# Attention in steps of a head pair: half-height score tiles, odd value windows copied on the chip, all local evacuations on ScalarE

## The chip, the cores and the metric

The kernel runs on one core of one Trainium2 chip. The metric is the device time of one execution in microseconds, as the median of several runs; the profile is one further execution, recorded by the hardware profiler. A core has TensorE (PE in the profile, with its weight loads as PEld), VectorE (DVE), ScalarE (ACT), GpSimd (POOL) and SyncE (SP), which issues the DMAs here. Matrix products go into PSUM, which has eight banks of 512 fp32 numbers per partition; PE writes them, and VectorE and ScalarE read them out ("evacuate" them) into SBUF.

## The reference

Eight batches of eight heads; 512 local and 32 global tokens; head dimension 64. Global queries attend to everything, local queries to the 32 global keys and to local keys at most 32 positions away. The result is reordered to 4352 rows of 512 and goes through a mixture of eight experts with a greedy assignment.

```python
s_g = scale * np.matmul(q_g, k_all.transpose(0, 1, 3, 2))
out_g = np.matmul(sm(s_g), v_all)
s_ll = scale * np.matmul(q_l, k_l.transpose(0, 1, 3, 2))
mask = np.abs(pos[:, None] - pos[None, :]) <= window      # window = 32
s_ll = np.where(mask, s_ll, -1000000000.0)
s_lg = scale * np.matmul(q_l, k_g.transpose(0, 1, 3, 2))
out_l = np.matmul(sm(np.concatenate([s_lg, s_ll], axis=-1)), np.concatenate([v_g, v_l], axis=2))
...
for e in range(E):                                        # after the greedy assignment
    h = np.maximum(x[mask] @ w1[e], 0.0)
    out[mask] = h @ w2[e]
```

`sm` is a softmax with the row's maximum subtracted.

## The kernel before

The program has two stages: `attention` (lines 64 to 376), which writes its result x to the DRAM tensor `xd` and the gate's logits to `L`, and then routing and `experts` (from line 687). Only the first stage and the host's layout of its inputs (`_layout`, line 961) are touched by the change.

The 512 local queries of a head are cut into 16 blocks (windows) of 32. With the global keys woven in between the local ones (`_blocks`), the keys that a block may see are 128 neighbouring columns, starting at 32 * ((3j + 1) // 2) for block j. So the scores of a block are a 32x128 tile. The host ships for each of the 32 (batch, head pair)s a tensor `qk` with the transposed queries (544 columns) and keys (864 columns) of two heads, one head on partitions 0 to 63 and one on 64 to 127, and a tensor `vw` with the values of all 16 windows of both heads, 128 keys on the partitions, 65 columns each (the 65th is ones and yields the softmax's sum). Neighbouring windows overlap, so most values are shipped more than once.

`load_qk` (line 75) loads q and k in two DMAs; `spread` (line 83) copies q into `qz`, in which the two heads' queries stand on the diagonal of zeros, so that one product over all 128 partitions gives the scores of one block of both heads (64 rows). GpSimd makes these copies, VectorE at the very start. `load_v` (line 89) loads the values in four DMAs.

The work is done in units. A `Local` unit is half of a head pair: eight blocks of both heads. A `Glob` unit is the 32 global queries of four heads. A unit has these parts:

- `a`: the scores. Local: eight products on 128x64 tiles of the array (two column halves, L136). Global: L197, of 512 and of 32 columns.
- `e`: the mask is added and the row maximum taken (VectorE, L143), the maximum is scaled by a small operation (L145), then the exponential (ScalarE, L147). Global: maxima L203 to L205, exponentials L212 to L218.
- `c`: the probabilities are transposed on PE (L152, global L226) into a bank called T, and `evac` copies them to SBUF; of each five copies (`nev`) three go to ScalarE (L253) and two to VectorE (L255).
- `d`: the outputs on 128x32 tiles (L164, global L236) into a bank called O, then VectorE divides by the sum (L167, L168, L172; global L239 to L243). After the last unit of a batch SP writes the batch to `xd` (L175); global rows go by L245.

PSUM is dealt out by names: S for scores with three banks, T with three, O with two. A tile of a name waits until the tile that had its bank three (or two) before was read.

The order is written out by hand. Line 340 runs over the units with a look-ahead of three: `a` and `e` of unit i + 3, `c` of unit i, `d` of unit i - 2; in even steps scores stand first and outputs last on PE, in odd steps the other way round, so that two units' scores and two units' outputs stand side by side. A batch has ten units: eight local and two global. Between them stand the gate's parts (`extra`): `gate_x` transposes x (L261), `gate_m` multiplies with the gate's weights (L267), `gate_l` transposes back and sums into `L` (L276, L277). Loads are issued up to four head pairs ahead; each engine's queue, SP's too, runs strictly in the order of the program, and a load waits on SP until its buffer is free. `rt.prepare` (line 432) makes tables for the routing on VectorE, once, early in attention.

Of the kernel before, what the change touches and what calls it, by code (L numbers as in the profile page):

```python
# [8 lines left out]
F32 = mybir.dt.float32  # L9
# [18 lines left out]
NZ = 6  # L28
# [36 lines left out]
def attention(ctx, tc, A, consts, xd, ident, L, nbatch, rt=None):  # L65
# [6 lines left out]
    G = [(b, g) for b in range(nbatch) for g in range(2)]  # L72
    qk, vw, xs = {}, {}, {}

    def load_qk(b, p):
        t = ld.tile([128, KW], F32, name="qk", bufs=5)
        q = ld.tile([128, QW], F32, name="q", bufs=3)
        z = qz[(b * NP + p) % NZ]
        nc.sync.dma_start(q, A["qk"][b, p, :, :QW])
        nc.sync.dma_start(t, A["qk"][b, p, :, QW:])  # L80
        qk[b, p] = t

        def spread(eng):
            for h in range(2):
                r = slice(64 * h, 64 * h + 64)
                eng.tensor_copy(z[r, :, h, :], q[r].rearrange("p (j i) -> p j i", i=32))  # L86
        return spread

    def load_v(b, p):
        t = ld.tile([128, 2, NW, D + 1], F32, name="vw", bufs=7)  # L90
        f, n = t.rearrange("p h w d -> p (h w d)"), NW * (D + 1) // 2
        for k in range(4):
            nc.sync.dma_start(f[:, k * n:k * n + n], A["vw"][b, p, :, k * n:k * n + n])
        vw[b, p] = t

    qz = [ac.tile([128, QW // 32, 2, 32], F32, name=f"qz{i}") for i in range(NZ)]
    pg = [ac.tile([128, 6, 128], F32, name=f"pg{i}") for i in range(3)]
    mask = ac.tile([128, 2 * NB, 128], F32, name="mask")
    wg = ac.tile([128, 4, 32], F32, name="wg")
    P = [(b, p) for b in range(nbatch) for p in range(NP)]  # L100

    warm = ac.tile([128, 128], F32, name="warm")
# [4 lines left out]
    for i in range(NZ):  # L107
        nc.gpsimd.memset(qz[i][64:128, :, 0, :], 0.0)
        nc.gpsimd.memset(qz[i][0:64, :, 1, :], 0.0)
    for i in range(3):  # L110
        nc.gpsimd.memset(pg[i], 0.0)
    load_qk(0, 0)(nc.vector)
    nc.sync.dma_start(mask.rearrange("p a b -> p (a b)"), A["mask"])
    nc.sync.dma_start(ident, A["ident"])
    spread1 = load_qk(0, 1)
    load_v(0, 0)
    nc.sync.dma_start(wg.rearrange("p a b -> p (a b)"), A["wg"])
    load_qk(0, 2)(nc.gpsimd)
    load_v(0, 1)

    class Local:
        def __init__(s, b, u):
            s.b, s.q, s.u = b, u // 2, u % 2

        def a(s):
            b, q = s.b, s.q
            z = qz[(b * NP + q) % NZ]
            kw = qk[b, q]
            st = ps.tile([128, NB, 128], F32, name="S", bufs=3)
            s.p = wk.tile([128, NB, 128], F32, name="p", bufs=5)  # L130
            s.nm = wk.tile([128, NB], F32, name="nm", bufs=6)
            for c in range(NB):
                for r in range(2):
                    j = 8 * s.u + 2 * c + r
                    k0 = 32 * ((3 * j + 1) // 2)
                    nc.tensor.matmul(st[64 * r:64 * r + 64, c, :], z[:, j].rearrange("p h i -> p (h i)"),  # L136
                                     kw[:, k0:k0 + 128], start=True, stop=True)
            s.st = st

        def e(s):  # L140
            st, nm = s.st, s.nm
            for c in range(NB):
                nc.vector.tensor_tensor_reduce(s.p[:, c, :], st[:, c, :], mask[:, 4 * s.u + c, :], 1.0, -BIG,  # L143
                                               ALU.add, ALU.max, nm[:, c:c + 1])
            nc.vector.tensor_scalar(nm, nm, -SCALE, None, op0=ALU.mult)  # L145
            for c in range(NB):
                nc.scalar.activation(s.p[:, c, :], s.p[:, c, :], AF.Exp, bias=nm[:, c:c + 1], scale=SCALE)  # L147
# [29 lines left out]
    class Glob:  # L177
        def __init__(s, b, g):
            s.b, s.g = b, g
# [845 lines left out]
```

## Time and profile before

| What | Value |
|---|---|
| median of 3 runs | 738.86 us (738.28 to 739.7) |
| the profiled execution's own time | 739.46 us |
| its span, first to last instruction | 737.7 us |
| mean granted TensorE clock | 0.972 |
| PE busy | 686.9 us (93%) |
| VectorE busy | 504.9 us (68%) |
| ScalarE busy | 313.6 us (43%) |
| GpSimd busy | 162.5 us (22%) |
| DMA moved | 120.53 MB, mean 163 GB/s |

A row of a timeline gives start and duration in microseconds, engine, line, operation, output<-inputs, shapes and how many instructions were merged; for a matrix product the shape is rows*columns of the array's tile and then partitions x columns of the moving operand. Durations of matrix products are modelled and overlap; from one run's start to the next one's is what a run costs PE. A fp32 product is two instructions on PE, a transpose is one. A row of a group of instructions gives busy microseconds and the mean nanoseconds of one, then the idle time of its engine before them and what ended it.

### The profile page before, as it was taken

The numbers are of one execution on the slowest core, as the hardware profiler recorded it, in microseconds if no ns is written. First come the engines' busy times: TensorE is split into PE (matmuls) and PEld (weight loads), VectorE is DVE, ScalarE is ACT, GpSimd is POOL, SyncE is SP. The second block draws the span as 40 slices with busy tenths as digits, with TensorE's granted clock in tenths as the row PEclk, the third lists the DMA queues.
The fourth block names the chain that finished last, engine by engine and source line by source line (L and its number), as shares of the span: only waits on it lengthen the run. The fifth ranks groups of instructions, "written<-read, shape, count | busy, mean of one in ns | idle before, by whom it ended". The sixth has DMA issues, their size and how long they took to land.

```text
span 737.7 us, 21308 instructions
## 1 busy us (share of the span) xinstructions
PE 686.9 (93%) x8672; PEld 564.7 (77%) x8672; DVE 504.9 (68%) x1848; ACT 313.6 (43%) x849; POOL 162.5 (22%) x191
## 2 busy tenths in 40 slices
PE   8889999999996279999999999999999999999997
PEld 7677777877773169768878978977977877987985
DVE  5887877977887788866777777776786865550410
ACT  4656756666662034234334333343332433541520
POOL 5222212212100040141042043034024025312002
PEclk9989999999998579999999999999999999999999
DMA  9988998999921061171081072054045055522001
GB/s 324 387 310 296 361 305 300 328 323 306 334 80 60 1 236 55 45 263 45 1 289 62 1 263 89 1 202 148 3 135 200 16 171 192 163 73 89 16 16 46
DMA packets 46242, 120.53 MB, mean 163 GB/s; under 512 B 8256, under 2 KB 8512, under 8 KB 42048
## 3 DMA queue, kind: packets, MB, share of 16 engines
q1 hardware_dynamic: 35904, 67.78, 26.5%
q0 software_dynamic: 10240, 51.39, 19.8%
q8 instruction: 68, 1.11, 0.6%
q14 instruction: 30, 0.25, 0.1%
HBM read 101.32 MB, written 17.83 MB: 162 GB/s over the span
## 4 chain that ended last, share of the span: by engine, by line
PE 45%; DVE 5%; DMA 2%; issue 2%; ACT 1%; POOL 0%; POOLq 0%; DVEq 0%; ACTq 0%
PE Y L903 21%; PE H L875 17%; PE R L485 3%; PE H L747 2%; DVE w2l L417 2%; PE Y L893 2%; DMA w1r<-in_w_dram,widx 1%; DVE r_G L417 1%; ACT w2h L724 1%; DMA xg<-xd,idx 1%; DVE hl L417 0%; DVE r_pm L417 0%; POOL xg L708 0%; PE Y L909 0%; DMA out_dram<-y,idx 0%
## 5 line engine op out<-in xcount | busy, mean ns | idle before, releaser
L875 PE MATMUL H<-xh,w1h 128*128 128x272 f32 x512 | 151.5, 296 | 1.8 <-DVE hl L417 1.4
L875 PE MATMUL H<-xh,w1l 128*128 128x272 f32 x512 | 150.0, 293 | 0.0
L875 PE MATMUL H<-xl,w1h 128*128 128x272 f32 x512 | 149.9, 293 | 0.0
L147 ACT ACTIVATE p<-p,nm 128x128 f32<-128x128 f32 x256 | 81.7, 390 | 65.9 <-DVE nm L145 54.1
L877 ACT ACTIVATE hh<-H 128x272 fp32r<-128x272 f32 x128 | 50.9, 398 | 130.2 <-PE H L875 125.8
L903 PE MATMUL Y<-w2h,hh 128*128 128x512 f32 x256 | 103.9, 406 | 0.0
L903 PE MATMUL Y<-w2l,hh 128*128 128x512 f32 x256 | 102.7, 401 | 0.0
L903 PE MATMUL Y<-w2h,hl 128*128 128x512 f32 x256 | 102.4, 400 | 0.0
L875 PEld LDWEIGHTS H<-xh,w1h 128*128 128x128 f32 x512 | 96.4, 188 | 5.2 <-DVE hl L417 2.4
L875 PEld LDWEIGHTS H<-xl,w1h 128*128 128x128 f32 x512 | 96.5, 188 | 0.6
L875 PEld LDWEIGHTS H<-xh,w1l 128*128 128x128 f32 x512 | 96.4, 188 | 0.3
L86 POOL COPY qz<-q 64x544 f32<-64x544 f32 x60 | 39.2, 654 | 150.3 <-DMA q<-in_qk_dram 108.1
L136 PE MATMUL S<-qk,qz 128*64 128x128 f32 x1024 | 68.5, 284 | 3.1 <-DVE qz L86 2.4
L754 POOL DMA_INDIRECT out_dram<-y,idx x40 | 41.1, 1027 | 136.4 <-ACT y L845 79.3
L417 DVE SCALAR_TENSOR_TENSOR hl<-H,hh 128x272 fp32r<-128x272 f32 x128 | 54.4, 433 | 23.6 <-ACT h L879 12.7
L143 DVE CUSTOM_DVE_ANT_0 p<-S,mask 128x128 f32<-128x128 f32 x256 | 58.8, 285 | 14.9 <-PE S L136 10.5
L417 DVE TENSOR_TENSOR w2l<-w2r,w2h 128x512 fp32r<-128x512 f32 x64 | 43.1, 686 | 37.3 <-ACT w2h L724 37.0
L136 PEld LDWEIGHTS S<-qk,qz 128*64 128x64 f32 x1024 | 58.5, 142 | 10.1 <-issue 6.6
L708 POOL DMA_INDIRECT w1r<-in_w_dram,widx x16 | 15.6, 977 | 221.1 <-DVE r_a L417 124.5
L845 ACT ACTIVATE y<-Y 128x512 f32<-128x512 f32 (+1 forms) x40 | 23.2, 594 | 91.9 <-PE Y L903 70.1
L903 PEld LDWEIGHTS Y<-w2h,hh 128*128 128x128 f32 x256 | 48.2, 188 | 15.7 <-issue 5.9
L724 ACT ACTIVATE w1h<-w1r 128x512 fp32r<-128x512 f32 x64 | 36.4, 622 | 50.4 <-DVE L L417 29.9
(168 smaller groups left out, 1205.9 us busy)
## 6 DMA issues: line engine op xcount, KB each, us to landing
vw<-in_vw_dram SPq DMA_DIRECT2D x128, 260.0 KB, 5.8
qk<-in_qk_dram SPq DMA_DIRECT2D x32, 432.0 KB, 5.8
q<-in_qk_dram SPq DMA_DIRECT2D x32, 272.0 KB, 5.2
xd<-xs SPq DMA_DIRECT2D x8, 1024.0 KB, 7.8
xd<-xg SPq DMA_DIRECT2D x64, 8.0 KB, 4.8
xg<-xd,idx POOLq DMA_INDIRECT x40, 3.6
out_dram<-y,idx POOLq DMA_INDIRECT x40, 2.8
mask<-in_mask_dram SPq DMA_DIRECT2D x1, 512.0 KB, 6.3
```

Of the source, the lines that this page charges most:

```text
L86: eng.tensor_copy(z[r, :, h, :], q[r].rearrange("p (j i) -> p j i", i=32))
L136: nc.tensor.matmul(st[64 * r:64 * r + 64, c, :], z[:, j].rearrange("p h i -> p (h i)"), kw[:, k0:k0 + 128], start=True, stop=True)
L143: nc.vector.tensor_tensor_reduce(s.p[:, c, :], st[:, c, :], mask[:, 4 * s.u + c, :], 1.0, -BIG, ALU.add, ALU.max, nm[:, c:c + 1])
L147: nc.scalar.activation(s.p[:, c, :], s.p[:, c, :], AF.Exp, bias=nm[:, c:c + 1], scale=SCALE)
L417: return op(*args, **kw)
L485: s.nc.tensor.matmul(out, *args, **kw)
L724: nc.scalar.activation(hi, raw, AF.Copy)
L754: nc.gpsimd.indirect_dma_start(out=out, out_offset=bass.IndirectOffsetOnAxis(ap=rt.idx[ph][:n, t:t + 1], axis=0), in_=y[:n], in_offset=None)
L845: nc.scalar.activation(y[:n], p[:n], AF.Copy)
L875: nc.tensor.matmul(p, w[d][:, fs], x[:, d, q], start=(d + k == 0), stop=(d + k == 5))
L877: nc.scalar.activation(hh[:, f, q], p, AF.Relu)
L903: nc.tensor.matmul(p, h[:, f, q], w[f], start=(f + k == 0), stop=(f + k == 9))
```

## The change

A unit becomes a whole head; the work goes in steps of a head pair (five steps to a batch: four local pairs and one of the two global units), with a look-ahead of two steps.

- Scores: `qz` and its copies go. Each head is multiplied for itself on tiles of 64 rows and 32 columns, the two heads alternating, each head into its own S bank: 32 products a pair in place of 16. The global scores are made the same way by `glob_scores`, 512 columns into two S banks, 32 columns into an S bank for the first head and a T bank for the second.
- Maxima: scores are scaled by -SCALE as the mask is taken and the minimum is kept, so that it is the bias of the exponential as it stands (which has scale -1); the small scaling operation goes. The mask is half as large, as a bank now holds one head.
- Values: the host ships the even windows alone, in two DMAs; the odd ones are put together by four GpSimd copies from the even ones, moved by 32 or 64 partitions.
- Evacuations: local and global transposes and the gate's product go to ScalarE, the gate's transposed x to VectorE.
- Buffers: seven for qk (queries and keys in one tile), seven for the values, seven for p, five for pt, and more for small tiles.
- Order within a step: loads; scores of step i + 2; transposes and evacuations of step i, head by head; masks and exponentials of step i + 2; outputs and normalisation of step i - 1; a gate part.

```diff
     def load_v(b, p):
-        t = ld.tile([128, 2, NW, D + 1], F32, name="vw", bufs=7)
-        f, n = t.rearrange("p h w d -> p (h w d)"), NW * (D + 1) // 2
-        for k in range(4):
-            nc.sync.dma_start(f[:, k * n:k * n + n], A["vw"][b, p, :, k * n:k * n + n])
+        t = ld.tile([128, 2, 2, NW // 2, D + 1], F32, name="vw", bufs=7)
+        ev, od = t[:, 0], t[:, 1]
+        n = NW // 2
+        for h in range(2):
+            nc.sync.dma_start(ev[:, h].rearrange("p w d -> p (w d)"), A["vw"][b, p, :, h * n * (D + 1):(h + 1) * n * (D + 1)])
+        nc.gpsimd.tensor_copy(od[0:64], ev[64:128])
+        nc.gpsimd.tensor_copy(od[64:96], ev[32:64])
+        nc.gpsimd.tensor_copy(od[96:128, :, :n - 1], ev[64:96, :, 1:])
+        nc.gpsimd.tensor_copy(od[96:128, :, n - 1:], ev[64:96, :, n - 1:])
         vw[b, p] = t
...
+        def mask(s):
+            s.p = wk.tile([128, NB, 128], F32, name="p", bufs=7)
+            s.nm = wk.tile([128, NB], F32, name="nm", bufs=8)
             for c in range(NB):
-                nc.vector.tensor_tensor_reduce(s.p[:, c, :], st[:, c, :], mask[:, 4 * s.u + c, :], 1.0, -BIG,
-                                               ALU.add, ALU.max, nm[:, c:c + 1])
-            nc.vector.tensor_scalar(nm, nm, -SCALE, None, op0=ALU.mult)
+                nc.vector.tensor_tensor_reduce(s.p[:, c, :], s.st[:, c, :], mask[:, c, :], -SCALE, BIG,
+                                               ALU.add, ALU.min, s.nm[:, c:c + 1])
+        def exp(s):
             for c in range(NB):
-                nc.scalar.activation(s.p[:, c, :], s.p[:, c, :], AF.Exp, bias=nm[:, c:c + 1], scale=SCALE)
+                nc.scalar.activation(s.p[:, c, :], s.p[:, c, :], AF.Exp, bias=s.nm[:, c:c + 1], scale=-1.0)
...
+    def local_scores(u):
+        t = qk[u[0].b, u[0].q]
+        for x in u:
+            x.st = ps.tile([128, NB, 128], F32, name="S", bufs=3)
+        for c in range(NB):
+            for r in range(4):
+                j = 4 * c + r
+                k0 = QW + 32 * ((3 * j + 1) // 2)
+                for h in range(2):
+                    e = slice(64 * h, 64 * h + 64)
+                    nc.tensor.matmul(u[h].st[32 * r:32 * r + 32, c, :], t[e, 32 * j:32 * j + 32], t[e, k0:k0 + 128],
+                                     start=True, stop=True)
...
+    def glob_scores(u):
+        b = u[0].b
+        for x in u:
+            x.sa = ps.tile([128, 512], F32, name="S", bufs=3)
+        for x, n, k in zip(u, "ST", (3, 3)):
+            x.sb = ps.tile([128, 32], F32, name=n, bufs=k)
...
+    nev = dict(p=0, g=0, x=0, l=0)
+    who = dict(p="A", g="A", x="D", l="A")
...
+    LA = 2
+    for i in range(-LA, ns + 1):
...
+        if nx:
+            (local_scores if isinstance(nx[0], Local) else glob_scores)(nx)
+        if cur:
+            cur[0].turn()
+        if cur:
+            cur[0].take()
+        if cur:
+            cur[1].turn()
+        if cur:
+            cur[1].take()
+        if nx:
+            nx[0].mask()
+        if nx:
+            nx[1].mask()
+        if nx:
+            nx[0].exp()
+        if nx:
+            nx[1].exp()
+        if old:
+            old[0].out()
+        if old:
+            old[0].norm()
+        if old:
+            old[1].out()
+        if old:
+            old[1].norm()
+        for f in extra.get((i, 0), []):
             f()
```

Here `nx`, `cur` and `old` are steps i + 2, i and i - 1.

## What was predicted before the run

> **What bounds the kernel now.** The page comes first: how long, which engine is busy, and where.
>
> ```profile
> span 737.7 us, 21308 instructions
> PE   8889999999996279999999999999999999999997
> DMA  9988998999921061171081072054045055522001
> ```
>
> A slice is 18.4 us. In the first twelve (0 to about 221 us) PE and the DMA engines are both at nine tenths; then follow the routing (a hole of PE) and the experts. The diff touches attention alone, so the rest is taken as unchanged. For attention's rhythm I read the timeline of SP's queue: one write of a finished batch to xd each time round.
>
> ```profile
> 75.53 0.38 SPq L175 DMA_DIRECT2D xd<-xs  x1
> ...
> 182.64 0.38 SPq L175 DMA_DIRECT2D xd<-xs  x1
> ```
>
> These are the second and the sixth of eight, so four batches took 107.1 us: **26.8 us a batch**. Whether PE or the loads set that is read from PE's own timeline inside one batch (start, duration, shape, count).
>
> ```profile
> 102.20 0.66 PE L152 MATMUL T<-ident,p 128*128 128x128 f32 x4
> 102.69 0.60 PE L261 MATMUL T<-ident,xs 128*128 128x128 f32 x4
> 103.22 1.97 PE L136 MATMUL S<-qk,qz 128*64 128x128 f32 x32
> 105.12 0.88 PE L226 MATMUL T<-ident,pg 128*128 128x128 f32 x6
> 105.92 1.11 PE L164 MATMUL O<-vw,pt 128*32 128x65 f32 x64
> 106.97 0.66 PE L152 MATMUL T<-ident,p 128*128 128x128 f32 x4
> ...
> 108.91 1.12 PE L197 MATMUL S<-qk,qz 128*64 128x512 f32 x8
> 109.96 0.66 PE L152 MATMUL T<-ident,p 128*128 128x128 f32 x4
> 110.55 0.88 PE L236 MATMUL O<-vw,pgt 128*32 128x64 f32 x48
> 111.25 0.64 PE L164 MATMUL O<-vw,pt 128*32 128x65 f32 x32
> ...
> 123.19 1.07 PE L267 MATMUL O<-xt,wg 128*32 128x512 f32 x8 [0.80 <-DVE gm L239]
> 124.19 1.17 PE L197 MATMUL S<-qk,qz 128*64 128x512 f32 x8
> ```
>
> Each run starts as the one before ends: PE is one dense chain, and the only long pause here is the 0.80 us that the row at 123.19 names. From start to start: scores of a pair (32 instructions) 1.90 us; eight transposes (102.20 to 103.22) 1.02; outputs of a pair (64) 1.05; a gate's four transposes 0.53; scores of one global unit 1.05; its transposes 0.80; its outputs 0.70; the gate's product 1.00. So **PE sets the batch**, and time taken out of PE's chain shortens it until the next engine is reached. The loads are close behind:
>
> ```profile
> DMA packets 23458, 44.52 MB, mean 318 GB/s; under 512 B 4293, under 2 KB 4293, under 8 KB 23425
> ...
> vw<-in_vw_dram SPq DMA_DIRECT2D x88, 260.0 KB, 5.6
> qk<-in_qk_dram SPq DMA_DIRECT2D x22, 432.0 KB, 5.2
> q<-in_qk_dram SPq DMA_DIRECT2D x22, 272.0 KB, 5.0
> ```
>
> That is the DMA view of 55 to 195 us. A pair loads 4 x 260 + 432 + 272 = 1744 KB.
>
> **The change part by part.** *Scores.* Before, a pair has 16 products on 128x64 tiles, two side by side, 32 instructions in 1.90 us. After, it has 32 products on 64x32 tiles: 64 instructions of the same 128 columns, over eight tiles. If all eight run side by side, 64 x (1.90/32) x 2/8 = 0.95 us. No row of this trace has a tile of fewer than 128 rows, so this is bounded: 0.95 from below (nothing makes one instruction shorter), 1.90 from above if only the four column tiles overlap and the row halves take turns. I take 1.05, the row of outputs: the same 64 instructions with 32-column weights. Global scores: two units at 1.05 become one run of half as many streamed columns per tile and twice the tiles, a quarter of 2.1, so 0.53, plus a start; I take 0.75 (bound 1.2).
>
> *The rest of PE's chain* is regrouped but not shortened: per pair 1.02 for transposes and 1.05 for outputs. Per batch PE then has four pairs at 1.05 + 1.02 + 1.05 = 3.12, so 12.5; the global step 0.75 + 2 x 0.75 (transposes) + 2 x 0.75 (outputs) = 3.75; the gate 4 x 0.6 (0.53 and a start, as each stands alone now) + 1.0 + 0.5 (four transposes back) = 3.9. Together **20.1 us**, against 26.8.
>
> *A new wait.* The small global scores of the second head now sit in a T bank, and T has three. That step also takes two T banks for its own transposes, and in it stands a gate unit's transposes, which need the fourth and so wait for ScalarE's last exponential of the second global head. ScalarE's rows give the price.
>
> ```profile
> 102.79 1.28 ACT L147 ACTIVATE p<-p,nm 128x128 f32<-128x128 f32 x4 [1.55 <-DVE ls L167]
> 103.97 0.57 ACT L253 ACTIVATE pt<-T 128x512 f32<-128x512 f32 x1
> 104.45 0.58 ACT L253 ACTIVATE xt<-T 128x512 f32<-128x512 f32 x1
> ...
> 112.37 0.56 ACT L212 ACTIVATE pg<-S,gm 128x384 f32<-128x384 f32 x1
> ...
> 113.53 0.60 ACT L253 ACTIVATE pt<-T 128x512 f32<-128x512 f32 x1
> ```
>
> An evacuation takes 0.48, a global unit's exponentials 1.16, four local ones 1.18. In that step PE has scores until 0.75, transposes until 1.8, outputs until 2.8, and then the gate. ScalarE evacuates until about 2.6 and exponentiates until 2.6 + 2 x 1.16 = 4.9; with the hops, the gate starts at 5.1 rather than 2.8. Behind it on PE stand the next pair's scores, so the chain waits **2.3 us** a batch (bounds 0 and 2.3; I take 2.3, since PE is in order). Then the batch is 20.1 + 2.3, and with 0.3 for pauses like today's **22.7**.
>
> *The engines that could take over.* ScalarE now evacuates all local and global transposes: per pair 2 x 1.18 + 2 x 0.48 = 3.3, four pairs 13.3, a global step 2 x 1.16 + 4 x 0.48 = 4.2, the gate 0.6: 18.1 a batch. For VectorE and GpSimd:
>
> ```profile
> L143 DVE CUSTOM_DVE_ANT_0 p<-S,mask 128x128 f32<-128x128 f32 x164 | 37.7, 286 | 6.6 <-PE S L136 5.4 <-ACT xt L253 1.2
> L86 POOL COPY qz<-q 64x544 f32<-64x544 f32 x40 | 25.5, 637 | 104.0 <-DMA q<-in_qk_dram 74.5 <-PE O L164 10.0 <-PE S L197 6.5
> L255 DVE COPY pt<-T 128x512 f32<-128x512 f32 x16 | 11.0, 686 | 3.3 <-PE T L152 2.9 <-PE T L261 0.4
> L203 DVE TENSOR_REDUCE gm<-S 128x1 f32<-128x512 f32 x10 | 6.9, 686 | 3.9 <-PE S L197 3.9
> ```
>
> ```profile
> 133.51 0.15 DVE L167 TENSOR_SCALAR ls<-O 128x4 f32<-128x4 f32 x1
> ...
> 134.25 0.15 DVE L167 TENSOR_SCALAR ls<-O 128x4 f32<-128x4 f32 x1
> ```
>
> VectorE: eight masks at 0.286 and two normalisations at 0.74 are 3.8 a pair, 15.1 for four; four gate copies 2.7; the global step 2 x (0.69 + 0.4 + 0.75), 3.7: 21.5 at most, since neighbours overlap. Its evacuations and the scaling of the maxima go; they were off PE's chain, so that gives room and no time. GpSimd: 544 elements took 0.637, 1.17 ns each; the four copies of a pair have 1040 + 1040 + 910 + 130 = 3120 elements a partition, 3.7 us, 14.6 a batch, beside PE and four pairs ahead of use. Were it later, outputs would wait. Bounds: 3.7, and twice that, since no copy here moves partitions. I take 3.7. The loads: 4 x 1224 KB, and 1088 KB for xd, are 6.1 MB, at 318 GB/s 19.3 us. SP also holds a value load until the global outputs free four tiles at once, some two steps; the next batch's need is three steps off. All stay under 22.7.
>
> *GpSimd against VectorE.* One VectorE operation shows what a GpSimd copy can do to it:
>
> ```profile
> L145 DVE TENSOR_SCALAR nm<-nm x64: 169/170/706, 9.1 to 219.4; 128x4 f32<-128x4 f32 x64
> ```
>
> Median 170 ns, worst 706, near the 637 of the qz copy that then runs. The change removes this operation, but `prepare` has over a dozen VectorE instructions inside SBUF, which now meet copies of 1.2 us. Bounds 0 and about 12 x 0.6 = 7 us, once; I take 2. The Trainium skill, "SBUF — State Buffer", section "Who interferes with whom", says that a VectorE copy or scalar operation in a two-port mode and a GpSimd instruction exclude each other for a whole instruction. By that rule the price is real and grows with copy length, near the upper bound; on the row above the trace agrees, though the median says that most are not hit.
>
> *Start.* Ahead of the third pair's qk go 256 KB less of mask and 520 KB less of values: 0.78 MB at 318 GB/s, 2.4 us earlier. The spreads and memsets of qz go too, hidden behind that. The tail's gate copies all go to VectorE: +0.5.
>
> **Sum.** Eight batches at 22.7 - 26.8 = -4.1: -32.8; start -2.4; prepare +2; tail +0.5: -32.7. On the profiled execution's own 739.46 us that gives 706.8; it stands 0.6 over the median of 738.86, so about 706.5. I say **707**.
>
> **The rivals.** *PE alone.* The T bank comes free in time or its wait is made up: the batch is 20.1, 2.3 x 8 = 18 us less plus pauses, **686**. For it: bounds as above; against: ScalarE's sum leaves little to make up with.
>
> *Row halves take turns.* The scores stay at 1.90 a pair and 1.2 for the global: +0.85 x 4 + 0.45 = +3.9, the batch is 26.6, **737**. Here the change does not do what it says. For it: no row shows two row tiles; against: column tiles do overlap, two in L136 and four in L164.
>
> *Evacuation binds.* If neighbours on ScalarE stop overlapping (0.39 for an exponential, 0.58 for a copy), its batch is 4 x (3.1 + 1.2) + 4.6 + 0.6 = 22.3, VectorE's 21.5, and engines that wait on one another in order lose some 10%: 24.5, **721**. The Trainium skill, "TensorEngine Tiling (Array Packing)", section "PSUM Bottleneck", says that tiling speeds up TensorE but not the copies out of PSUM, and advises both engines for them; the change goes to one. Today's trace can't show it, as PE is the bound.
>
> *GpSimd binds, slower than before.* If copies to other partitions take 2.2 times the qz rate, a pair needs 8.0 us, a batch 32, and outputs wait for odd tiles: +5.2 x 8, **780**. It decides from 26.8/4 = 6.7 us a pair, 1.8 times. Against it: the qz copies hardly vary, and start and end on quarters of the partitions as these do.
>
> **How the numbers follow.** A measurement can tell about 0.2%, 1.5 us. Chances: forecast 0.50 (696 to 718), PE alone 0.14, evacuation 0.14, row halves 0.12 (a third of it within 0.2%), GpSimd 0.07, some other slower wait 0.03. Faster 0.86, same 0.04, slower 0.10. The range reaches from PE alone, 684, to row halves, 737: about 0.17 stay outside.
>
> **What would show it.** Right: in PE's timeline a pair's 64 score instructions take about 1.05 us start to start; xd writes come 22.7 us apart; once a batch PE pauses some 2 us before the gate's transposes, with ScalarE's exponentials as the releaser; GpSimd copies of about 1.2 us. Wrong: score runs of 1.9; PE pausing at outputs for GpSimd; ScalarE without gaps; SP holding loads so long that scores wait for qk.

## The result, and the profile after

The changed kernel takes 743.84 us (median of 20 runs, 740.12 to 748.0), the kernel before 738.96 us on the same chip (20 runs, 736.99 to 742.07): a ratio of 1.0071, 95% interval 1.0055 to 1.0086. It is **slower by 0.7%**, where 707 us were forecast. Below, the top of its page, with PE's and the DMA engines' slices.

```profile
span 742.2 us, 23504 instructions
PE 667.9 (90%) x9824; PEld 543.8 (73%) x9824; DVE 480.3 (65%) x1762; ACT 320.1 (43%) x867; POOL 220.2 (30%) x247
PE   7788889888697259999999999999999999999997
DMA  9665864876622052081072063044035044522001
```

Attention still fills the first twelve slices. But PE, mostly at nine tenths there before, is now mostly at eight, and the DMA engines fell from nine tenths, after the first slice, to between two and eight. No engine is full, and the stage is no shorter. SP's timeline gives the second and the sixth write of a batch:

```profile
73.66 1.35 SPq L157 DMA_DIRECT2D xd<-xs  x1
...
182.49 0.56 SPq L157 DMA_DIRECT2D xd<-xs  x1
```

(182.49 - 73.66) / 4 is 27.2 us a batch, against 26.8 before and 22.7 forecast. So the expected gain is not given back later; it does not show in these four batches. The first batch is written sooner than before (46.06 us for 50.53), and from the first write to the last it takes 186.7 us (to 232.80) for 179.9 (to 230.43). PE's timeline of one stretch says where it goes:

```profile
98.55 0.87 PE L169 MATMUL S<-qk 64*32 64x128 f32 x40
99.99 0.64 PE L169 MATMUL S<-qk 64*32 64x128 f32 x24 [0.56 <-issue]
100.56 1.09 PE L132 MATMUL T<-ident,p 128*128 128x128 f32 x8
101.58 1.12 PE L143 MATMUL O<-vw,pt 128*32 128x65 f32 x64
102.63 0.66 PE L274 MATMUL T<-ident,xs 128*128 128x128 f32 x4
...
104.13 0.22 PE L248 MATMUL T<-qk 64*32 64x32 f32 x3
105.88 0.26 PE L248 MATMUL T<-qk 64*32 64x32 f32 x5 [1.53 <-issue]
106.06 1.09 PE L132 MATMUL T<-ident,p 128*128 128x128 f32 x8
107.09 1.12 PE L143 MATMUL O<-vw,pt 128*32 128x65 f32 x64
108.14 0.66 PE L274 MATMUL T<-ident,xs 128*128 128x128 f32 x4
108.82 1.17 PE L169 MATMUL S<-qk 64*32 64x128 f32 x46
111.80 0.62 PE L169 MATMUL S<-qk 64*32 64x128 f32 x18 [1.81 <-issue]
```

Where nothing stops them, the runs are as short as forecast: transposes 1.02 (100.56 to 101.58), outputs 1.05 (101.58 to 102.63), transposes again 1.03. But three runs are cut in two, in the middle of a loop over products of the same kind, by waits that no semaphore ended: the profile calls them "issue". The view of PE's waits from 55 to 195 us sums them up (total us, times, longest):

```profile
PE S L169 <- issue: 9.8, 10, 2.4
PE O L143 <- issue: 5.4, 5, 2.2
PE T L274 <- issue: 2.6, 2, 1.8
PE O L223 <- issue: 2.1, 3, 1.3
PE T L248 <- issue: 1.5, 1, 1.5
PE T L132 <- issue: 1.3, 1, 1.3
```

Together 22.7 us. The same view of the kernel before has three such rows, all of them:

```profile
PE S L136 <- issue: 0.5, 1, 0.5
PE O L236 <- issue: 0.2, 1, 0.2
PE O L164 <- issue: 0.2, 1, 0.2
```

That is 0.9 us. What PE lacks in these waits is instructions. The page's list of DMA queues has one marked "instruction" (packets, MB, share), here of the kernel after and then of the kernel before:

```profile
q8 instruction: 77, 1.26, 0.7%
```

```profile
q8 instruction: 68, 1.11, 0.6%
```

After, PE runs 9824 products and 9824 weight loads: 19648 / 77 is 255 a packet. Before, 17344 / 68 is 255 too. So a packet is a block of some 255 PE instructions: 1.26 MB / 77 is 16 KB, 64 bytes an instruction. And the waits sit on its borders: counted through the trace, the 15 waits on "issue" of over 0.8 us that PE's weight loads have between 55 and 195 us end 2.1 to 2.8 us after such a packet started, and all of them at instruction 170 to 174 of a period of 254. The change lowers PE's work per batch and raises its instructions, from 1136 to 1424 loads and products.

How late a block comes is seen at 99.99 us, where PE reaches one. First SP's timeline there, three rows of a stretch in which it issues ten loads and the write of a batch without a pause; then the list of queues in two windows of the DMA view:

```profile
97.59 1.36 SPq L84 DMA_DIRECT2D vw<-in_vw_dram  x2
...
100.95 0.41 SPq L157 DMA_DIRECT2D xd<-xs  x1
...
102.67 1.43 SPq L84 DMA_DIRECT2D vw<-in_vw_dram  x2
```

```profile
q1 hardware_dynamic: 425, 0.98, 96.8%
```

```profile
q1 hardware_dynamic: 155, 0.29, 83.5%
q8 instruction: 1, 0.02, 4.2%
```

The first window is 100 to 103.4 us: data only, and no instruction packet for 3.4 us. The second is 103.4 to 104.8: the packet is there, and PE goes on at 105.88, 5.9 us after it reached the block before. The Trainium skill, "Runtime: NRT & Kernel Launch", section "Instruction fetch mechanics", says that an engine fetches the next 16 KB page while it executes the current one, and that this is mostly hidden. By the rows the first half holds here; the second held before the change and not after it.

### The profile page after: what moved, and what is told of

The parts are those of the page before. It is cut to its first block, busy times and chain, and to the rows that moved or that the text cites. A ratio compares the mean times of both kernels' runs of the same rounds, so it can differ in the third digit from the quotient of the medians.

```text
span 742.2 us, 23504 instructions
## 1 busy us (share of the span) xinstructions
PE 667.9 (90%) x9824; PEld 543.8 (73%) x9824; DVE 480.3 (65%) x1762; ACT 320.1 (43%) x867; POOL 220.2 (30%) x247
## 3 DMA queue, kind: packets, MB, share of 16 engines
q8 instruction: 77, 1.26, 0.7%
## 4 chain that ended last, share of the span: by engine, by line
PE 77%; DVE 10%; issue 6%; DMA 4%; ACT 2%; SPq 0%; POOLq 0%; POOL 0%; DVEq 0%; ACTq 0%
PE Y L931 22%; PE H L903 21%; PE S L169 6%; PE T L132 5%; PE O L143 4%; PE R L513 4%; PE H L775 2%; DVE r_G L445 2%; PE T L274 2%; DVE w2l L445 2%; PE T L205 2%; PE Y L921 2%; PE O L223 2%; DMA qk<-in_qk_dram 1%; PE T L280 1%
## 5 line engine op out<-in xcount | busy, mean ns | idle before, releaser
L122 DVE CUSTOM_DVE_ANT_0 p<-S,mask 128x128 f32<-128x128 f32 x256 | 56.7, 286 | 40.9 <-PE S L169 40.8
L127 ACT ACTIVATE p<-p,nm 128x128 f32<-128x128 f32 x256 | 78.0, 397 | 7.5 <-DVE nm L122 7.5
L445 DVE SCALAR_TENSOR_TENSOR hl<-H,hh 128x272 fp32r<-128x272 f32 x128 | 54.4, 433 | 23.5 <-ACT h L907 12.7
L85 POOL COPY vw<-vw 64x1040 f32<-64x1040 f32 x32 | 33.5, 1047 | 109.3 <-DMA vw<-in_vw_dram 90.9
L873 ACT ACTIVATE y<-Y 128x512 f32<-128x512 f32 (+1 forms) x40 | 23.2, 594 | 92.3 <-PE Y L931 70.6
L169 PE MATMUL S<-qk 64*32 64x128 f32 x2048 | 47.3, 300 | 15.5 <-issue 12.0
L931 PEld LDWEIGHTS Y<-w2h,hh 128*128 128x128 f32 x256 | 48.2, 188 | 15.8 <-issue 5.9
L266 ACT ACTIVATE pt<-T 128x512 f32<-128x512 f32 x64 | 35.6, 596 | 55.4 <-PE T L132 55.1
L752 ACT ACTIVATE w1h<-w1r 128x512 fp32r<-128x512 f32 x64 | 36.4, 622 | 49.9 <-DVE L L445 30.3
```

The lines of the kernel that those rows point to most:

```text
L85: nc.gpsimd.tensor_copy(od[0:64], ev[64:128])
L122: nc.vector.tensor_tensor_reduce(s.p[:, c, :], s.st[:, c, :], mask[:, c, :], -SCALE, BIG, ALU.add, ALU.min, s.nm[:, c:c + 1])
L169: nc.tensor.matmul(u[h].st[32 * r:32 * r + 32, c, :], t[e, 32 * j:32 * j + 32], t[e, k0:k0 + 128], start=True, stop=True)
L266: nc.scalar.activation(dst, src, AF.Copy)
L445: return op(*args, **kw)
L752: nc.scalar.activation(hi, raw, AF.Copy)
```

## The experiments

The ratio of each is to the kernel before on the same chip, as chips differ by 1% (the kernel before took 738 to 746 us on them).

**Without most loads, the first time** (few_loads). The theory at this point was F: PE's blocks come at a fixed rate at best. The rival D: the loads hold them up.

The edit in `load_qk`, for pairs 7 to 24, and likewise for the loads in `load_v`:

```diff
+        no, k = again(b, p)
+        if no:
+            qk[b, p] = qk[k]
+            return
...
```

> The changed kernel, with the loads of pairs 7 to 24 left out: those pairs compute on the tiles of the pair seven before them, and every instruction of the five engines stays. Theory F (PE runs dry of instructions: they come in blocks of some 254, at most one block in about 3.5 us, whatever the data queues do): PE's waits that nothing released ("issue") between 55 and 195 us stay near 20 us (22.7 in the changed kernel), a batch stays at 26 to 27.5 us, the time at 735 to 748. Rival D (the instruction blocks come late because the loads fill the DMA engines): these waits fall below 6 us, the batch to 21 to 24 us, the time to 695 to 720.

Ratio 0.9981 (0.9955 to 1.0007), far from what D gave for the time. The run was uneven. GpSimd's copies onto tiles in use held the start up (they waited 11.8 us for outputs up to 76 us; second batch written at 75.03 us), and the loads came back near 130 us. Between, without loads, the batches were written at 75.03, 96.09, 118.42 and 139.73 us, 21.6 apart; the next two took 34.3 and 29.6. Two windows of the quick stretch (busy us and count of PE, PEld, VectorE, ScalarE, GpSimd; granted clock; DMA share; GB/s):

```profile
82.00:109.00 27.00, 25.95 (x856) 20.01 (x844) 22.62 (x125) 22.35 (x71) 16.53 (x21) 1.00 0.15 48
109.00:136.00 27.00, 26.74 (x922) 20.83 (x921) 23.72 (x136) 23.10 (x77) 16.21 (x20) 1.00 0.26 83
```

PE's waits on "issue" are 1.2 us from 82 to 136 us, with all of GpSimd's copies still running. So D is right there and F in its plain form falls. The theory became FD: PE asks for a block as it reaches the one before, and a block takes 3.5 us to come, more behind loads. The trace's packets agree: within attention the smallest distance of two was 3.3 to 3.5 us in every kernel of this study.

**Less work in each instruction** (half_outputs).

```diff
-                    nc.tensor.matmul(s.o[32 * r:32 * r + 32, c, :], s.pt[:, c, 32 * r:32 * r + 32],
-                                     vw[b, q][:, r % 2, h, 2 * c + r // 2, :], start=True, stop=True)
+                    nc.tensor.matmul(s.o[32 * r:32 * r + 32, c, 32:], s.pt[:, c, 32 * r:32 * r + 32],
+                                     vw[b, q][:, r % 2, h, 2 * c + r // 2, 32:], start=True, stop=True)
...
```

> The changed kernel, but each local output product computes 33 columns instead of 65 (half of a head's outputs and the sum; the half is written twice): as many PE instructions, less work in each. An unstalled run of 64 should fall from 1.05 us to 0.6 to 0.9 us, 0.6 to 1.8 us a batch. Theory F: the block sets the pace, so little of that comes through: batch 26.5 to 27.5 us, time 738 to 747. Rival A (the length of PE's work sets the batch): the batch is shorter by all that the runs lose, time 729 to 738.

Ratio 1.0074 (1.0050 to 1.0098), the same as the changed kernel's 1.0071; the batch is 27.8 us ((184.88 - 73.54) / 4), with 23.2 us of waits on "issue". A run of outputs without a wait fell from 1.05 to 0.72 us (100.83 to 101.55), 1.3 us a batch, and none of that reached the time. The clock is a rival here: it was granted at 0.88 to 0.94 in four of the five windows of 27 us from 55 to 190 us, against 0.94 in three in the changed kernel, an estimated 1.1 us a batch more. So this run alone doesn't show that PE's work does not set the batch.

**The same instructions in another order** (spread_scores).

```diff
...
-            (local_scores if isinstance(nx[0], Local) else glob_scores)(nx)
+            loc = isinstance(nx[0], Local)
+            local_scores(nx, range(0, 2)) if loc else glob_scores(nx)
         if cur:
             cur[0].turn()
         if cur:
             cur[0].take()
+        if nx and loc:
+            local_scores(nx, range(2, 4))
```

> The changed kernel with the same instructions in another order: half of a pair's scores, four transposes, the other half, four transposes, so that the 128 short instructions of the scores don't stand in one run. Theory F: a burst takes fewer instructions from the block in hand before transposes let the next one come, so waits on "issue" fall by some 5 us between 55 and 195 us, batch 25.5 to 27 us, time 728 to 742. Rival B (waits on banks and on ScalarE, the order of the step): VectorE gets its scores later, batch 27 to 28.5 us, time 743 to 755.

Ratio 1.0115 (1.0057 to 1.0172). The waits on "issue" fell to 13.4 us, as F and FD expect, and yet the batch stayed at 27.0 us ((180.43 - 72.49) / 4): the batch and the time are those of rival B. Only 2.0 us of PE's waits for others stand in their place, but PE was busy for 23.9 of 27 us from 55 to 190 us, 22.9 in the changed kernel, and in one window the clock was 0.88. How these add up was not tried, so the run settles nothing by itself.

**Fewer instructions** (outputs_bf16).

```diff
-        t = ld.tile([128, 2, 2, NW // 2, D + 1], F32, name="vw", bufs=7)
+        ev = ld.tile([128, 2, NW // 2, D + 1], F32, name="ve", bufs=7)
+        t = ld.tile([128, 2, 2, NW // 2, D + 1], BF16, name="vw", bufs=7)
...
-            s.pt = wk.tile([128, NB, 128], F32, name="pt", bufs=5)
+            s.pt = wk.tile([128, NB, 128], BF16, name="pt", bufs=5)
...
```

> The changed kernel with probabilities and values of all output products in bfloat16 (GpSimd's copies convert, one copy more a pair): a product is then two PE instructions instead of four, 1072 a batch instead of 1424. Theory F: demand falls under the supply, waits on "issue" between 55 and 195 us fall from 22.7 to under 8 us, the batch to 21 to 23.5 us, time 700 to 722. Rival A or B: only what the output runs themselves lose comes through (at most 0.5 us a pair, 2 us a batch), time 727 to 740. Rival P (GpSimd binds at some 4.4 us a pair): batch not under 25 us, with outputs waiting for GpSimd.

Ratio 0.9705 (0.9650 to 0.9759), batch 22.9 us ((179.33 - 64.97) / 5), as F and FD expect, with GpSimd at 4.4 us a pair. The waits on "issue" are 13.9 us, more than the 8 expected; that the quicker batch asks for blocks nearly as often may be why. But the output runs lost more than the expectation allowed for: a pair's take 0.36 us (103.03 to 103.39) for 1.05, a batch's global ones 0.48 (112.55 to 113.03) for the 1.5 of the prediction, together 3.8 us a batch of the 4.3 gained. So this run agrees with FD and doesn't tell it from rival A.

**No loads at all, after the first seven pairs** (no_loads).

Now for all later pairs, GpSimd's copies too:

```diff
+        return i >= 7, P[i % 7 if i < 28 else 34 - i]
...
+        if no:
+            vw[b, p] = vw[k]
+            return
```

> The changed kernel, where only the first seven pairs are loaded and copied and all later pairs compute on their tiles: the loads and GpSimd's copies after them are left out, the other engines' instructions stay. Theory FD (PE reaches a block of 254 instructions, only then asks for the next one, and that one comes 3.5 us later without other traffic, up to 6.5 us later behind loads): without loads a batch is 21 to 22.5 us all through, waits on "issue" of PE between 55 and 195 us under 5 us, time 692 to 712. Theory F (the rate of blocks alone, whatever the loads do): batch 26 to 27.5 us, 735 or more. Rival A2 (few_loads' quick batches came from something else than the loads): no steady 21 to 22.5 us.

Ratio 0.9626 (0.9561 to 0.9691), 711.86 us. Batches were written at 61.94 and 173.05 us, five apart: **22.2 us**. Its windows, with the changed kernel's behind it (busy us and count of PE, PEld, VectorE, ScalarE, GpSimd; granted clock; DMA share; GB/s):

```profile
55.00:82.00 27.00, 26.21 (x907) 20.47 (x899) 22.87 (x138) 22.77 (x72) 0.00 (x0) 1.00 0.14 46
136.00:163.00 27.00, 26.40 (x870) 20.51 (x860) 23.34 (x130) 22.40 (x72) 0.00 (x0) 1.00 0.14 46
```

```profile
82.00:109.00 27.00, 23.73 (x717) 18.13 (x717) 18.38 (x107) 17.23 (x54) 12.34 (x16) 0.94 0.65 218
136.00:163.00 27.00, 24.90 (x761) 18.99 (x753) 19.65 (x112) 17.59 (x55) 15.03 (x18) 0.94 0.75 257
```

These are two of five windows from 55 to 190 us. Over all five PE is busy for 25.7 of 27 us without loads (95%) and for 22.9 with them (85%), and a sixth fewer products fit in. The clock stays at 1.00 without loads; with them it is 0.94 in three windows, as it stands at half speed for 3.4 us at a time, for example at 113.0 to 116.4 us, after PE's wait of 1.81 us. A step without loads looks as the prediction had it:

```profile
97.01 1.41 PE L181 MATMUL S<-qk 64*32 64x128 f32 x64
98.35 1.09 PE L144 MATMUL T<-ident,p 128*128 128x128 f32 x8
99.38 1.12 PE L155 MATMUL O<-vw,pt 128*32 128x65 f32 x64
100.42 0.66 PE L286 MATMUL T<-ident,xs 128*128 128x128 f32 x4
101.01 1.16 PE L181 MATMUL S<-qk 64*32 64x128 f32 x64
102.10 1.78 PE L217 MATMUL T<-ident,pg 128*128 128x128 f32 x12
```

A pair's scores are 1.09 here (101.01 to 102.10), and waits on "issue" between 55 and 195 us are 5.1 us, at the edge of what FD expected.

**More loads: the odd values by DMA again** (odd_by_dma).

```diff
-        nc.gpsimd.tensor_copy(od[0:64], ev[64:128])
...
+        for k in range(4):
+            nc.sync.dma_start(f[:, k * n:k * n + n], A["vw"][b, p, :, k * n:k * n + n])
```

> One part of the change undone: the odd value tiles come by DMA as before (1744 KB a pair instead of 1224) and GpSimd copies nothing. Theory FD: more traffic ahead of the instruction blocks, so more waits on "issue" (25 to 45 us between 55 and 195 us against 22.7), batch 27.5 to 30 us, time 745 to 775. Rival P (GpSimd's copies are what holds the changed kernel up): batch under 25 us, time under 730. Rival F (rate of blocks alone): unchanged, 738 to 748.

Ratio 1.0328 (1.0254 to 1.0402). The batch is 30.5 us ((203.54 - 81.57) / 4), the waits on "issue" 24.7. So GpSimd's copies don't hold the changed kernel up; put in place of these loads they save it 2.5% (1.0328 / 1.0071). Of the 3.3 us that the batch grew, the waits on "issue" make 1.0 (5.4 us a batch for 4.4); PE also waited 7.7 us for DMAs and ScalarE, which it did not in the changed kernel, some 1.7 a batch. So more loads cost time in both ways. From the trace's packets between 55 and 195 us, the middle time from the instruction that reaches a block to the start of the next packet was 1.0 us without loads, 2.4 in the changed kernel (1.7 to 2.7, depending on which of the instructions 170 to 174 is counted as the block's first) and 2.9 with the odd values by DMA.

**The score tiles alone, in the kernel before** (before_64x32).

```diff
-                    nc.tensor.matmul(st[64 * r:64 * r + 64, c, :], z[:, j].rearrange("p h i -> p (h i)"),
-                                     kw[:, k0:k0 + 128], start=True, stop=True)
+                    for h in range(2):
+                        e = slice(64 * h, 64 * h + 64)
+                        nc.tensor.matmul(st[64 * r + 32 * h:64 * r + 32 * h + 32, c, :], z[e, j, h], kw[e, k0:k0 + 128],
+                                         start=True, stop=True)
```

> One part of the change alone: the kernel before, in its own order and with all its loads, with the local scores on 64x32 tiles (twice as many instructions of the same columns, 256 more a batch). Rival A (PE's work sets the batch): the pair's scores fall from 1.90 to 1.05 us, the batch from 26.8 to 23.4 to 24.5 us, time 708 to 722. Theory FD (a block of 254 instructions then lasts 4.3 us of work and comes up to 6.5 us later behind loads that fill the DMA engines by nine tenths): the gain goes into waits on "issue", batch 26 to 29 us, time 733 to 757.

Ratio 1.0313 (1.0243 to 1.0383), and at unchanged work of the scores, which was not meant:

```profile
112.46 1.95 PE L138 MATMUL S<-qk,qz 64*32 64x128 f32 x64
114.34 0.87 PE L228 MATMUL T<-ident,pg 128*128 128x128 f32 x6
...
117.22 0.85 PE L138 MATMUL S<-qk,qz 64*32 64x128 f32 x20
119.70 0.63 PE L138 MATMUL S<-qk,qz 64*32 64x128 f32 x12 [1.64 <-issue]
```

A pair's scores take 1.88 us (112.46 to 114.34), not 1.05: this edit uses only four of the eight tiles. Head h stands on row half h and on column tile 2r + h, so each head has two column tiles and neither uses the other's. By the prediction's own sum that is 64 x (1.90/32) x 2/4 = 1.90 us. In the trace these products start in groups of four, 0.02 us wide and 0.11 us apart; in the changed kernel in groups of eight, 0.05 us wide and 0.11 us apart. So this kernel has the work of the kernel before and 256 instructions more a batch, and it loses 3.1%: the batch is 29.9 us ((199.90 - 80.32) / 4) for 26.8, with 15.8 us of waits on "issue" for 0.9, which is 3.4 us a batch for 0.2. **Instructions alone cost that.** The Trainium skill, "TensorEngine Tiling (Array Packing)", section "Gotcha 1: PSUM Pressure", says that different row tiles cannot use one PSUM bank at the same time. Here the two row halves write into one bank, each in its own column tiles, and their products start together; in turns, two at a time, they would need 3.8 us by the same sum, so the measurement differs from the page.

**The score tiles undone, in the changed kernel** (scores_128x64).

```diff
-                for h in range(2):
-                    e = slice(64 * h, 64 * h + 64)
-                    nc.tensor.matmul(u[h].st[32 * r:32 * r + 32, c, :], t[e, 32 * j:32 * j + 32], t[e, k0:k0 + 128],
-                                     start=True, stop=True)
+                    nc.tensor.matmul(x.st[64 * r:64 * r + 64, c, :], z[:, j].rearrange("p h i -> p (h i)"),
+                                     kw[:, k0:k0 + 128], start=True, stop=True)
```

> One part of the change undone: the local scores go back to products of 128 rows and 64 columns on the spread query tile (32 PE instructions a pair instead of 64 to 1.90 us, GpSimd spreads the queries again, one buffer less for some tiles); the order, ScalarE's evacuations and GpSimd's odd values stay. Theory FD: 1168 weight loads and products a batch over 23.5 us of work, so a block of 254 lasts 5.1 us and the next one (3.5 to 6.5 us) is mostly there in time: waits on "issue" 5 to 14 us between 55 and 195 us, batch 24 to 25.5 us, time 712 to 730, faster than both kernels. Rival A (PE's work counts, as forecast): this part costs 0.85 us a pair, slower than the changed kernel by 20 us or more. Rival (the order, ScalarE or GpSimd holds the changed kernel up): about as slow as it, 738 to 750.

Ratio 1.0338 (1.0275 to 1.0401). Of FD's numbers one came true, the waits on "issue" (6.6 us), and the times did not: by the ratios it is 2.7% slower than the changed kernel (1.0338 / 1.0071), some 20 us, which is what rival A gave. PE's other waits from 55 to 195 us show a part of it:

```profile
PE S L275 <- DVE nm L140: 2.9, 1, 2.9
...
PE S L188 <- POOL qz L89: 2.2, 2, 1.9
```

The spread tiles left room for fewer buffers, and GpSimd stood in the way at times; and PE's work was more than the 23.5 us that I had summed up (it was busy for 24.8 of 27 us from 82 to 190 us, on average), so the batch was 27.4 us ((196.02 - 86.60) / 4). It isn't a clean undoing. It says that fewer instructions mean fewer such waits, and it leaves open whether the work that the small tiles save counts as rival A has it.

**The values alone, in the kernel before** (before_pool_odd). The diff is that of `load_v` in the section on the change.

> One part of the change alone: the kernel before in its own order, with the odd value tiles copied by GpSimd (1224 KB of loads a pair instead of 1744). Theory FD: PE's stream there is slow enough that its instruction blocks come in time, so lighter traffic helps little: batch 25.8 to 26.8 us (26.8 before), the start some 2 to 5 us earlier, time 726 to 738. Rival D (whatever lightens the loads helps by itself): batch under 25.5 us, under 724. Rival P (GpSimd's copies hold VectorE or the outputs up): batch over 27 us, 742 or more.

Ratio 1.0070 (1.0044 to 1.0096): the copies helped nothing there. The waits on "issue" are 0.8 us, as FD expects of PE's slower stream. But the batch of 27.2 us and the loss are rival P's numbers and not FD's: from 55 to 195 us PE waited 4.2 us for VectorE's `gm` (2.2 before), and VectorE was busy for 22.5 of 27 us (21.9 before). The gain expected at the start came and went: the first batch was written at 41.53 us for 50.53, the second at 75.64 for 75.53, and the next four batches took 27.2 us each ((184.46 - 75.64) / 4). What made the second batch so long was not tried.

**The loads paced** (paced_loads, then paced_loads2). From pair 7 on each load waits for a VectorE memset of one element at its place in the step.

```diff
...
+            if tick:
+                nc.vector.memset(t[0:1, q][:, 0:1], 0.0)
...
```

> The changed kernel with the same loads spread evenly: from pair 7 on each of a pair's four loads waits for a one-element VectorE memset that stands at its place in the step (four places a step), so that no more than one load or two stand in the queues at once, instead of bursts of up to ten. Theory FD: an instruction block then waits for one load at most (1.2 to 2.2 us to its start instead of up to 4), waits on "issue" fall from 22.7 to 5 to 12 us between 55 and 195 us, batch 22.5 to 25 us, time 705 to 728. Rival (the sum of the traffic counts, not its bunching): batch 26 to 27.5 us, 735 to 748. Rival (the memsets hold VectorE up, or loads come too late): scores or outputs wait for DMA, batch over 27.5 us.

Ratio 1.0097 (1.0058 to 1.0136). The batches up to 142.59 us were 26.0 apart on average ((142.59 - 38.69) / 4), then 30 to 32. The last pair's loads now came too late: after 190 us PE waited 3.3 us for its qk and 4.4 for its values. Why the two batches from 142.59 us on took 30.3 and 31.0 us already was not tried.

> The paced loads again, but the last pair's loads no longer wait for a memset and stand one step earlier (in the run before, the end of attention waited 3.3 us for its qk and 4.4 us for its values). Theory: only these late loads go, 5 to 9 us, time 735 to 742, the batches in the middle stay at 25 to 27 us and waits on "issue" at 14 to 18 us between 55 and 195 us, since one load at a time still stands ahead of the instruction blocks. Rival (bunching is the cause after all and was hidden by the late loads): under 730.

Ratio **0.9940** (0.9909 to 0.9972): with only those last loads moved, it is faster than the kernel before and, by the ratios, 1.3% faster than the changed kernel. The middle batches are 25.8 us by the second and the sixth write ((165.93 - 62.90) / 4) for 27.2, the waits on "issue" 17.6 us, the middle time to a packet's start 1.9 us for 2.4 (1.7 to 1.9, counted the other ways). So in the middle bunching is a part of it, and the smaller one. But the last two batches took 27.4 and 32.1 us, for 29.5 and 20.8 in the changed kernel, and from the first write to the last it takes 188.6 us for 186.7. What is gained by then, 7.4 us, stems from the first batch, written at 36.85 us for 46.06; why that one came sooner was not tried.

**The end of attention** (paced_tail). In the changed kernel VectorE runs the routing's first operations ahead of the last normalisations and gate copies, and PE waits for these:

```profile
233.43 0.69 PE L274 MATMUL S<-ident,gx 128*128 128x128 f32 x2 [3.15 <-DVE xt L268]
```

```diff
-        for f in extra.get((i, 2), []):
+        for n, f in enumerate(extra.get((i, 2), [])):
             f()
-        if rt and i >= ns - 1:
+            if rt and i == ns and n == 4:
+                for _ in range(12):
+                    next(first, None)
+        if rt and i >= ns:
...
```

> The paced loads of the run before with one edit at the end of attention: the routing's first VectorE operations, which in the changed kernel stand ahead of the last gate copies (PE waited 3.15 us for these copies), are issued between the last step's gate copies and its gate sums. Theory: the end of attention is a chain of its own (7.0 us from the last normalisation to the last gate sum in the changed kernel, 4.4 before), so 1.5 to 3 us go: ratio to the kernel before 0.988 to 0.993, time 729 to 741 by the chip. Rival (the clock that falls to half speed there sets that time, not the order): within 1 us of the run before, ratio 0.993 to 0.996.

Ratio 0.9941 (0.9917 to 0.9966), as without the edit. From the last batch's write to the end of the last gate sum it took 5.4 us (225.84 to 231.26) for 7.1 (225.43 to 232.49), so the edit is worth 1.7 us there; but the waits on "issue" were 21.2 us for 17.6, and the sum doesn't show it. In these stretches the granted clock was 1.00 for 0.53, so the order and the clock, the rival, changed together, and the run doesn't tell them apart.

## Why the prediction was wrong

**The step that failed** is the one that adds PE's runs up to a batch: "Together 20.1 us, against 26.8", then "the batch is 20.1 + 2.3", 22.7. It took for granted that PE has its instructions when it needs them. The sum counted what each instruction does and not how many there are. At 1424 a batch in 20.1 us, 254 instructions last 3.6 us, and the next block needs 3.5 us at its best; before, 1136 in 26.8 us gave it 6.0. So 0.85 us saved on a pair's scores was bought with the instructions that take it back. That this is the cause is shown by no_loads (same PE stream, 22.2 us a batch), by the quick stretch of few_loads (the same with GpSimd's copies, 21.6) and by before_64x32 (no less work, more instructions, 3.1% lost). half_outputs (less work, no gain) and outputs_bf16 (fewer instructions and less work, 3.0% won) agree with it and don't show it by themselves.

Of the 5.0 us between 27.2 and 22.2, the waits on "issue" make some 3.6: 22.7 us over the 5.1 batches of 140 us, less 5.1 over 6.3. About 1.0 is the clock, an estimate: 0.94 for 1.00 in three of the five windows of 27 us from 55 to 190 us is 1.6 us each, over five batches. The rest I did not split.

**What held.** The sizes: scores 1.09 (1.05 forecast), transposes 1.02, outputs 1.05; tiles of 64 rows in two banks do run side by side, so the rival of row halves in turns falls, though its 737 us is the nearest of all to the time, by luck. GpSimd's copies, 3.3 us a pair (3.7 forecast), from the groups of 28 to 200 us:

```profile
L86 POOL COPY vw<-vw 32x1040 f32<-32x1040 f32 x25 | 26.2, 1048 | 1.0
...
L87 POOL COPY vw<-vw 32x910 f32<-32x910 f32 x26 | 24.5, 941 | 1.1
```

So "GpSimd binds" falls: copies to other partitions cost 1.0 ns an element, no more than the copies of qz before. "Evacuation binds" falls too: without loads PE is busy for 95% of the time, on the same evacuations.

**What was mis-sized.** PE's runs come to some 21.2 us a batch (22.2 without loads, less 0.95 of waits) for 20.1; the global scores are the largest part of that, 1.11 us (114.08 to 115.19 without loads) for 0.75. The wait on the T bank, 2.3 us a batch, is not there: the gate's transposes (L274) waited for instructions alone, and all that PE's weight loads waited for ScalarE's exponentials at the small scores (L248) is 1.4 us from 55 to 195 us, five times 0.3. The bank comes free in time, as in the rival of PE alone. VectorE's tables in `prepare` (2 us forecast) show one stretched operation, the copy of 128x8 at L495 with 684 ns for 120 before, some 0.6 us, near the lower bound. The start and the first batch were forecast to gain 6.5 us together (2.4 + 4.1), and the first write came 4.5 us sooner. The end of attention cost 2.6 us (0.5 forecast), from the last normalisation to the last gate sum: 7.0 us at a granted clock of 0.54, for 4.4 at 1.00. This is VectorE's last gate sum after, and then before:

```profile
239.50 0.29 DVE L290 TENSOR_REDUCE L<-T 128x32 f32<-128x128 f32 x1 [1.20 <-PE T L289]
```

```profile
234.53 0.29 DVE L277 TENSOR_REDUCE L<-T 128x32 f32<-128x128 f32 x1 [1.15 <-PE T L276]
```

The last sum ends 5.0 us later (239.79 for 234.82), of which 2.4 had gathered by the last batch's write (232.80 for 230.43). From there on both profiled executions take the same 502 to 503 us. Two readings in the prediction are wrong and change nothing: among the experts, L747 has 32 products on tiles of 32 rows and 128 columns, so there is a row with fewer than 128 rows, but it shows no two row tiles side by side; and the range names 684 us for PE alone, where 686 was worked out.

**What was missing among the rivals** is the supply of instructions. The page of before had its numbers, 68 packets and 17344 instructions, and a batch had 42 instructions a microsecond that the change was to raise to 71. No row of before says that a limit lies at the upper one.

## What to carry to other kernels

Count PE's instructions a microsecond before splitting products into smaller tiles: here a block of 255 came every 3.5 us at best, and behind loads every 4.7 us on average (30 packets from 55 to 195 us) or 5.4 (26, with the odd values by DMA). So this stage, meant for 71 instructions a microsecond while it loads at 230 GB/s, reached 52. Waits that the profile puts down to "issue" in the middle of a run of equal products, at equal counts of instructions, were the sign of it. What helped here was less traffic, and fewer instructions with less work in them; loads spread over the step helped in the middle of attention and not at its end.

## What the runs showed of the hardware that was not expected

- An instruction block starts to come 1.0 us (middle) after PE reaches the one before it when no loads run, 1.7 to 2.7 us after it in the changed kernel and 2.9 with the odd values by DMA; where PE waits for it, it goes on 2.2 to 2.7 us after the packet's start. Within attention packets were never closer than 3.3 us.
- In the kernel before, at 42 instructions a microsecond, data traffic at 0.92 to 0.94 of the DMA engines' time left 0.9 us of such waits; in the changed kernel, at 71 forecast and 52 reached, traffic at 0.64 to 0.75 left 22.7.
- Products on tiles of 64 rows and 32 columns: 64 instructions of 128 columns take 1.09 us over eight tiles (no_loads) and 1.88 over four (before_64x32). Two row halves that write into one bank, in different columns of the array, run side by side.
- In the changed kernel the granted clock fell to half for 3.4 us at a time within attention, between 55 and 195 us each time after PE had waited 1.8 to 2.4 us (at 82.3, 113.0, 136.9 and 194.9 us) and not after its waits of up to 1.5. That isn't a rule: in before_64x32 no such fall followed a wait of 2.74 us at 99.30. Without loads the clock stayed at 1.00 from 55 to 190 us.
